# Retention and a multiplicative feed-forward block on one core: the copy of a w3 w_out tile placed behind the next tile's exponents, and the last tile of results stored in two halves

## The chip, the cores and the metric

The kernel runs on one core of a Trainium2 chip. The core has five engines with a queue of instructions each, which run side by side and wait for one another by semaphores: TensorE (PE, matmuls; its weight loads, PEld, are listed apart), VectorE (DVE), ScalarE (ACT), GpSimd (POOL) and SyncE (SP, which here issues DMAs). An instruction waits at the head of its engine's queue, and what stands behind it waits too. SBUF is the core's working memory, PSUM holds the results of matmuls in eight banks.

The metric is the device time of one execution in microseconds (us); lower is better. Inputs and outputs are in the chip's memory (HBM).

## The reference

All numbers are float32, except that the four weight matrices come as float64.

```python
scores = scale * np.matmul(q, k.transpose(0, 1, 3, 2))       # q, k, v: (8, 8, 576, 64)
rel = pos[:, None] - pos[None, :]
Dmat = np.where(rel >= 0, gamma[:, None, None] ** rel[None, :, :], 0.0)
attn = np.matmul(scores * Dmat[None], v)
x = np.ascontiguousarray(attn.transpose(0, 2, 1, 3)).reshape(B * S, H * D)   # (4608, 512)
a = x @ w1                    # w1, w2: (512, 1024)
b = x @ w2
h = a * b @ w3                # w3: (1024, 1024)
out = h @ w_out               # w_out: (1024, 512)
```

`h @ w_out` is `(a * b) @ (w3 @ w_out)`, so the kernel multiplies w3 by w_out once and uses the product, w3o (1024 x 512), for all tokens.

## The kernel before, in words

The kernel is written with a schedule by hand: each engine executes its instructions in the order in which the program issues them. Four kinds of work are interwoven.

**Attention** runs in 20 steps g (four pairs of batch entries, five chunks of the sequence each): loads of q, k and v, scaling by the decay on POOL (`scale`, L214, and `scale_blocks`, L191), transposes, scores, a running state, and `pv`, which writes tokens as columns of x^T.

**Weights.** A float64 weight arrives as pairs of 32-bit integers and is rebuilt as float32 by DVE and ScalarE, block by block. `begin_block` takes out the exponent (L370) and the mantissa (L374, L377) on DVE and has ScalarE turn the exponent into a factor with two activations (L380, L381). `end_block` puts the sign to it (L391, which needs ScalarE's result) and multiplies (L402), both on DVE. These steps are a generator, `conversion`, which begins a block before it ends the one before; `convert(n)` takes up to n steps of it, and `convert_up_to(n)` goes on until n blocks are done. A tile of w3 is two blocks; when the second is done, DVE also transposes the tile (L406) into w3T, which has three buffers. A block that has been ended makes room among five buffers for the load of a later one (`load_block`, on SP).

**The product w3 w_out** is made in eight tiles of 128 rows. `w3_mm(ft)` does tile ft: eight matmuls (each shows as two PE instructions) of w3T with `wo` into a PSUM bank `ps`, and then ScalarE's copy of the bank into `w3o` (L454). It is called from the loop at L733. While that loop has products of the first tokens to do (`todo`), they are mixed in; after that an iteration of the loop converts what is left of tile ft, calls `w3_mm(ft)`, and takes eleven more steps of conversion, which is a tile's worth. The banks `acc` are a ring of seven.

**Tokens.** `up` computes a * b for 192 positions of two batch entries in one quarter of the hidden width at a time by a Strassen scheme (seven products, whose sums DVE adds from PSUM, L502; L523 multiplies a by b). `down(x, y)` multiplies two tiles of 128 tokens, x above and y below, by w3o, in the same scheme: product 1 (A11 B11), 7 (S3 T3), 2, 6 (S2 T2), 5, 4 and 3 in this order, with sums added on DVE (L607) into `ot`, which has one buffer. S3, S2 and S1 are made on DVE at L569, L573 and L575, S4 at L628. The sums of w3o that `down` needs (T3, T2, T1, -T4) are made once, at L540, by `w3_sums`, spread over the first `up` after the product is finished. `put(m, t, row)` puts the store of one tile of tokens in a list (a tile that crosses an edge at 192 rows is stored in two pieces), and `store` issues what is listed on SP (L648). `down` calls `put` for y after product 4 and for x after product 3.

After the w3 stage, `open_attention` reuses the memory of the weight buffers, so the first loads of the next pair of batch entries wait on SP until the conversion is done. `work(n)` takes n items from the list of ups and downs; the last call, L843, empties it.

Of the kernel before, what the change touches and what calls it, by code (L numbers as in the profile page):

```python
# [40 lines left out]
def kernel(  # L41
# [13 lines left out]
    nc = tc.nc  # L55
# [3 lines left out]
    DM = H * D  # L59
    DF = moe_w3.shape[0]  # L60
    CV = 512
    P = 128
# [6 lines left out]
    NC = (S + P - 1) // P  # L69
# [3 lines left out]
    G = NB2 * NC  # L73
# [31 lines left out]
    live = {}  # L105
# [99 lines left out]
    def scale(g, nm, scalar=False):  # L205
        c = g % NC
        sz = sizes[c]
        t, gam = live[nm, g], {"q": gq, "v": gk}[nm]
        t = t[:sz].rearrange("p (b h) d -> p b h d", b=2)
        if scalar:  # L210
            for h in range(H):
                nc.scalar.mul(t[:, :, h, :], t[:, :, h, :], gam[:sz, c, h:h + 1])
            return
        nc.gpsimd.tensor_tensor(  # L214
            out=t, in0=t, in1=gam[:sz, c].unsqueeze(1).unsqueeze(3).to_broadcast([sz, 2, H, D]), op=ALU.mult)
# [214 lines left out]
    def go_on():  # L430
        while converting:
            r = next(converting[-1], "end")
            if r != "end":
                return r
            converting.pop()
        return "end"

    def convert(n):

        for _ in range(n):  # L440
            if go_on() is not None:
                return

    def convert_up_to(n):
        while converted[0] < n:
            assert go_on() is None


    def w3_mm(ft):
        ps = acc.tile([P, DM], F32, tag="acc", name="ps")  # L450
        for g in range(KF):
            nc.tensor.matmul(ps, live["w3T", ft][:, g, :], live["wo"][:, g, :],  # L452
                             start=(g == 0), stop=(g == KF - 1))
        nc.scalar.copy(live["w3o"][:, ft, :], ps)  # L454
        multiplied[0] += 1

    every = [(i, n) for i in range(NB2) for n in range(NB)]

# [123 lines left out]
    def ahead(x, y, n=3):  # L582
        todo_sums = pair_of(x, y)[2]
        for _ in range(min(n, len(todo_sums))):
            aside.append(todo_sums.pop(0))

    def down(x, y, then=None):
        for m, t in (x, y):
            if t == 2 and m % 2 == 0 and m > 0:
                assert (m, t) in carried  # L590
        a, done, left = pair_of(x, y)
        ahead(x, y)
        while len(done) < 3:
            aside.pop(0)()
        if then:
            ahead(*then)
        ps = {}
        ot = pools["ot"].tile([P, 2, 2, DM // 2], F32, tag="ot", name="ot")

        def product(nm, A, B, on=None):  # L600
            ps[nm] = ps[on] if on else acc.tile([P, DM // 2], F32, tag="acc", name="po")
            for f in range(NP):
                nc.tensor.matmul(ps[nm], a[A][:, f, :], live["W"][B][:, f, :], start=(f == 0 and not on),  # L603
                                 stop=(f == NP - 1), skip_group_check=True)

        def plus(nm, to, sb):
            nc.vector.tensor_add(ot[:, to[0], to[1]], ps[nm], ot[:, sb[0], sb[1]])  # L607

        def put(m, t, row):

            i, n = every[m]
            r0 = t * P
            while r0 < (t + 1) * P:
                b = r0 // TB
                e = min((b + 1) * TB, (t + 1) * P)
                r = (2 * i + b) * S + n * TB + r0 - b * TB
                stores.append((out[r:r + e - r0, :],
                               ot[r0 - t * P:e - t * P, row].rearrange("p h d -> p (h d)")))
                r0 = e
            if not keep_stores:  # L620
                store()

        C11, C12, C21, C22 = (0, 0), (0, 1), (1, 0), (1, 1)
        product(1, "A11", "B11")
        nc.scalar.copy(ot[:, 0, 0], ps[1])  # L625
        product(7, "S3", "T3")
        product(2, "A12", "B21", on=1)
        nc.vector.tensor_tensor(out=a["S4"], in0=a["A12"], in1=a["S2"], op=ALU.subtract)  # L628
        product(6, "S2", "T2")
        plus(6, C12, C11)  # L630
        nc.scalar.copy(ot[:, 0, 0], ps[2])
        plus(7, C21, C12)
        product(5, "S1", "T1")
        plus(5, C22, C21)
        product(4, "A22", "-T4")
        plus(4, C21, C21)
        put(*y, 1)
        product(3, "S4", "B22", on=5)
        while aside:
            aside.pop(0)()  # L640
        plus(3, C12, C12)
        put(*x, 0)

    stores, keep_stores = [], []

    def store():
        while stores:
            nc.sync.dma_start(*stores.pop(0))  # L648
# [83 lines left out]
    todo = [(0, 1, 2), (0, 0, 3), (0, 1, 3)] + [(0, 2, fp) for fp in range(NQ - 1)]  # L732
    while multiplied[0] < KF:  # L733
        ft = multiplied[0]
        done = at["w3", ft, DF // CV - 1] + 1
        ready = converted[0] >= done
        if todo:
            first = converted[0] < 4 * NQ
            up(*todo.pop(0), conv=2 if first else 1)
            convert(0 if first else 3)  # L740
        if ready or not todo:
            convert_up_to(done)
            w3_mm(ft)
        if not todo:
            convert(11)
    w3_part.close()


# [5 lines left out]
    ahead((2, 0), (2, 1), 1)  # L754
    up(0, 2, NQ - 1)
    down((2, 0), (2, 1), ((0, 0), (0, 1)))
    carry(2, 2)
    weights_part.close()
# [4 lines left out]
    keep_stores.clear()  # L763
    store()
    todo = [(down, (0, 0), (0, 1)), (down, (1, 0), (1, 1)), (down, (0, 2), (1, 2))]

    def add_pair(i):

        for n in range(NB):
            m = every.index((i, n))  # L770
            if m != NB:
                todo.append((up, i, n, 1))
            if m > NB and m % 2 == 0:
                todo.append((down, (m - 2, 2), (m - 1, 2)))
            todo.extend((up, i, n, fp) for fp in range(2, NQ))
            if m + 1 < len(every):
                todo.append((up, *every[m + 1], 0))
                if m % 2 == 0:
                    todo.append((carry, m, 2))
            else:  # L780
                todo.append((down, (m - 1, 2), (m, 2)))
            todo.append((down, (m, 0), (m, 1)))

    def work(n):
        for _ in range(min(n, len(todo))):
            fn, *args = todo.pop(0)

            nxt = next((x for x in todo if x[0] is not carry), None)
            if nxt and nxt[0] is down and fn is not carry:
                if fn is down:  # L790
                    args.append(nxt[1:])
                else:
                    last = args == [*every[max(nxt[1][0], nxt[2][0])], NQ - 1]
                    ahead(*nxt[1:], 1 if last else 3)
            fn(*args)

    scale(NC, "q")
    scale(NC, "v")
    front(NC)
# [4 lines left out]
    for g in range(NC, G):  # L804
        c = g % NC
        n = -(-len(todo) // (NC - c))
        if g + 2 < G and not in_blocks[g + 2]:
            load(g + 2, "k")
            load_blocks(g + 2, "q")
        if g + 1 < G:  # L810
            scale(g + 1, "v")
            if not in_blocks[g + 1]:
                front(g + 1, "k")
                front_blocks(g + 1, "q")
        half = (n + 1) // 2
        if in_blocks[g + 1]:
            scale_blocks(g + 1)
            work(1)
            front_blocks(g + 1)
            half = max(half - 1, 0)  # L820
        if in_blocks[g + 2]:
            load_blocks(g + 2, "q")
            load_blocks(g + 2, "k")
        work(half)
        pv(g)

        if g + 2 < G:
            queue = nc.scalar if in_blocks[g + 2] else nc.sync
            load(g + 2, "v", queue)
            if in_blocks[g + 2] and (g + 2) % NC != NC - 1:  # L830
                load(g + 2, "k", queue)
        if g + 1 < G:
            state(g + 1)
            score(g + 1)
        if g + 2 < G and not in_blocks[g + 2]:
            scale_blocks(g + 2)
        if g == NC + 1:
            strassen_tokens(1, 0)
            todo.extend((up, 1, 0, fp) for fp in range(2))
        work(n // 2)  # L840
        if c == NC - 1:
            add_pair(g // NC)
    work(len(todo))  # L843


# [41 lines left out]
```

## Time and profile before

The median of 12 runs is 863.88 us (862.36 to 865.34). The profiled execution took 862.98 us; its span, from the first to the last instruction, is 861.2 us.

| what | value |
|---|---|
| median of 12 runs | 863.88 us |
| profiled execution: own time, span | 862.98 us, 861.2 us |
| granted TensorE clock | 1.000 |
| w3 w_out stage, first to last matmul | 157.8 to 216.8 us |
| ScalarE's copies L454 in it | 8, of 587 ns |
| ScalarE's activations L380, L381 | 719 and 725 ns |
| DVE's L370, L374, L377, L391, L402 | 405, 418, 692, 687, 692 ns |
| DVE's transpose L406 | 1244 ns |
| stores of results, 256 KB and 128 KB | 24 and 24; 2.0 and 2.3 us from issue to landing |

A profile is read like this: a row of the page's groups names a line of the kernel, an engine, an operation, what it writes and reads, how many there are, their busy time and mean duration, and the idle time of the engine before them with what ended it ("<-ACT e L381": a semaphore of that instruction). The chain of waits follows the execution back from its end, at each step to what released the instruction. The work of engines that wait for something else costs no time, so the question is always which wait ends last. A matmul's end is modelled, and the mean of 596 ns for L452 counts overlapped time: they follow one another faster than that.

### The profile page before, as it was taken

What the parts mean: (1) busy time and instruction counts of PE and PEld (TensorE: products, weight loads), DVE (VectorE), ACT (ScalarE), POOL (GpSimd) and SP (SyncE); (2) the same over time, 40 slices, a digit from 0 to 9 for tenths busy, and PEclk for the clock granted to TensorE, in tenths of its full rate; (3) what the DMA queues carried; (4) which work ended last, traced back from release to release, by engine and by line L of the source; (5) the groups of instructions that cost most, each with busy time, mean ns of one, the idle gap of its engine ahead of it and who ended that gap; (6) DMA issues with size and microseconds to landing.
All of it is one profiled execution on the core that took longest, in us unless ns stands there. A gap on an engine that the chain in (4) does not pass through costs nothing.

```text
span 861.2 us, 15290 instructions
## 1 busy us (share of the span) xinstructions
PE 841.1 (98%) x6269; PEld 766.1 (89%) x6269; DVE 472.4 (55%) x794; ACT 182.1 (21%) x364; POOL 115.8 (13%) x96
## 2 busy tenths in 40 slices
PE   5899999999999999999999999999999999999998
PEld 5899999544888999999999999999999999999996
DVE  4898998986655344553544453535453334335343
ACT  3676333343122111101101101101101100001000
POOL 3010020001214213203023120230300101000000
PEclk9999999999999999999999999999999999999999
DMA  9993453455247524415241526061200000000001
GB/s 197 225 218 110 99 99 98 126 142 74 39 89 147 105 49 82 85 37 111 36 83 31 86 43 115 13 115 24 51 26 26 2 25 1 26 25 1 25 1 49
DMA packets 204918, 63.21 MB, mean 73 GB/s; under 512 B 186920, under 2 KB 195112, under 8 KB 204848
## 3 DMA queue, kind: packets, MB, share of 16 engines
q1 hardware_dynamic: 172208, 54.07, 30.3%
q10 hardware_dynamic: 32640, 8.16, 5.1%
q8 instruction: 49, 0.80, 0.4%
q14 instruction: 21, 0.17, 0.1%
HBM read 52.76 MB, written 9.44 MB: 72 GB/s over the span
## 4 chain that ended last, share of the span: by engine, by line
PE 83%; DVE 5%; DMA 2%; issue 2%; SPq 1%; ACT 1%; DVEq 0%; ACTq 0%
PE up L497 44%; PE po L603 24%; PE ps L452 4%; PE xps L300 3%; PE sc L243 3%; PE xps L293 2%; PE st L265 1%; DMA ld_q<-in_q_dram 1%; DVE c L502 1%; SPq L725 1%; PE tp L228 1%; DVE e L391 1%; DVE w L402 1%; DVE w3T L406 0%; DVE ab L523 0%
## 5 line engine op out<-in xcount | busy, mean ns | idle before, releaser
L502 DVE TENSOR_TENSOR c<-up,c 128x384 f32<-128x384 f32 x240 | 133.1, 555 | 184.8 <-PE up L497 180.1
L497 PE MATMUL up<-xT,wA 128*128 128x192 f32 x1152 | 212.1, 327 | 0.7 <-ACT xT L305 0.7
L497 PEld LDWEIGHTS up<-xT,wA 128*128 128x128 f32 x1152 | 190.7, 190 | 3.4 <-ACT xT L305 1.0
L497 PE MATMUL up<-T,wS 128*128 128x192 f32 x768 | 140.6, 326 | 2.1 <-DVE T L471 2.1
L497 PEld LDWEIGHTS up<-T,wS 128*128 128x128 f32 x768 | 127.3, 190 | 2.4 <-issue 2.4
L603 PE MATMUL po<-w3o,ab 128*128 128x256 f32 x456 | 104.3, 380 | 0.3 <-ACT ot L625 0.3
L603 PEld LDWEIGHTS po<-w3o,ab 128*128 128x128 f32 x456 | 85.8, 190 | 12.5 <-ACT ot L625 0.7
L607 DVE TENSOR_TENSOR ot<-po,ot 128x256 f32<-128x256 f32 x90 | 38.2, 424 | 75.4 <-PE po L603 72.6
L497 PE MATMUL up<-xT,wS 128*128 128x192 f32 x384 | 70.6, 327 | 0.6 <-DVE c L502 0.5
L517 ACT COPY c<-up 128x384 f32<-128x384 f32 x48 | 23.0, 479 | 226.4 <-PE up L497 222.2
L497 PE MATMUL up<-T,wA 128*128 128x192 f32 x384 | 70.2, 326 | 0.0
L246 DVE TENSOR_TENSOR pm<-sc,mask 128x512 f32<-128x512 f32 (+1 forms) x80 | 45.5, 628 | 44.8 <-PE sc L243 44.8
L603 PE MATMUL po<-wB,forms 128*128 128x256 f32 x288 | 65.2, 379 | 0.4 <-DVE forms L573 0.4
L497 PEld LDWEIGHTS up<-xT,wS 128*128 128x128 f32 x384 | 63.6, 190 | 1.5 <-DVE c L502 1.5
L497 PEld LDWEIGHTS up<-T,wA 128*128 128x128 f32 x384 | 63.7, 190 | 0.0
L603 PEld LDWEIGHTS po<-wB,forms 128*128 128x128 f32 x288 | 54.6, 190 | 8.2 <-PE po L603 0.8
L214 POOL TENSOR_TENSOR ld_v<-ld_v,gk 128x1024 f32<-128x1024 f32 (+1 forms) x17 | 33.1, 1945 | 197.8 <-DMA ld_v<-in_v_dram 161.5
L452 PE MATMUL ps<-wo,w3T 128*128 128x512 f32 x128 | 56.1, 596 | 2.9 <-DVE w3T L406 2.9
L452 PEld LDWEIGHTS ps<-wo,w3T 128*128 128x128 f32 x128 | 23.8, 190 | 34.5 <-issue 30.6
L471 POOL TENSOR_TENSOR T<-xT,T 128x384 f32<-128x384 f32 x20 | 20.8, 1042 | 218.4 <-PE up L497 216.7
L523 DVE TENSOR_TENSOR ab<-c 128x768 f32<-128x768 f32 x48 | 47.0, 978 | 3.8
L510 ACT COPY c<-up 128x384 f32<-128x384 f32 x48 | 22.9, 478 | 118.3 <-PE up L497 69.7
(73 smaller groups left out, 799.0 us busy)
## 6 DMA issues: line engine op xcount, KB each, us to landing
raw<-in_moe_w_dram SPq DMA_DIRECT2D x64, 128.0 KB, 3.0
bl_q<-in_q_dram SPq DMA_DIRECT2D x208, 32.0 KB, 2.1
out_dram<-ot SPq DMA_DIRECT2D x24, 256.0 KB, 2.0
bl_k<-in_k_dram SPq DMA_DIRECT2D x136, 32.0 KB, 2.2
raw<-in_moe_w_dram SPq DMA_DIRECT2D x8, 512.0 KB, 7.9
raw<-in_moe_w_dram SPq DMA_DIRECT2D x16, 256.0 KB, 7.1
ld_k<-in_k_dram SPq DMA_DIRECT2D x8, 512.0 KB, 7.0
ld_v<-in_v_dram SPq DMA_DIRECT2D x8, 512.0 KB, 7.2
```

Source lines behind the costliest of these rows:

```text
L214: nc.gpsimd.tensor_tensor(out=t, in0=t, in1=gam[:sz, c].unsqueeze(1).unsqueeze(3).to_broadcast([sz, 2, H, D]), op=ALU.mult)
L243: nc.tensor.matmul(sc[j][:sz, p, :sz], kT[hs, b, p, :sz], qT[hs, b, p, :sz], start=True, stop=True)
L246: nc.vector.tensor_mul(pm[:sz, b, j, :, :sz], sc[j][:sz, :, :sz], mask[:sz, :sz].unsqueeze(1).to_broadcast([sz, NP, sz]))
L300: nc.tensor.matmul(banks[r][heads[half], b, n, :sz], vs[:sz, b * H + 2 * p + j, :], pm[:sz, b, j, p, :sz], start=(c == 0 and m == 0), stop ...
L452: nc.tensor.matmul(ps, live["w3T", ft][:, g, :], live["wo"][:, g, :], start=(g == 0), stop=(g == KF - 1))
L497: nc.tensor.matmul(ps[:, w, :], a[:, w, r, :], b[:, r, :], start=(new and w == r == 0), stop=(w == r == 1), skip_group_check=True)
L502: nc.vector.tensor_add(c[:, to], ps, c[:, sb])
L510: nc.scalar.copy(c[:, 0], p1)
L517: nc.scalar.copy(c[:, 0], p1)
L523: nc.vector.tensor_mul(ab[:, 4 * fp:4 * fp + 4, :], c[:, :, 0, :], c[:, :, 1, :])
L603: nc.tensor.matmul(ps[nm], a[A][:, f, :], live["W"][B][:, f, :], start=(f == 0 and not on), stop=(f == NP - 1), skip_group_check=True)
L607: nc.vector.tensor_add(ot[:, to[0], to[1]], ps[nm], ot[:, sb[0], sb[1]])
```

## The change

`w3_mm` no longer issues the copy of its bank; it returns a function that does. The loop calls that function after the eleven steps of conversion, so the copy stands behind the instructions of those steps on ScalarE's queue. While `todo` has items, there are no such steps, and the copy is issued right after the matmuls.

`put` gets a parameter that selects columns. In the very last `down`, marked by `last=True`, the left half of x's columns is put (and so stored) after y, ahead of product 3, and the right half after product 3. In every other `down` nothing changes. The assignments to `g` serve to tell the last call.

```diff
@@ w3_mm
         for g in range(KF):
             nc.tensor.matmul(ps, live["w3T", ft][:, g, :], live["wo"][:, g, :],
                              start=(g == 0), stop=(g == KF - 1))
-        nc.scalar.copy(live["w3o"][:, ft, :], ps)
         multiplied[0] += 1
+        return lambda: nc.scalar.copy(live["w3o"][:, ft, :], ps)
@@ down
-    def down(x, y, then=None):
+    def down(x, y, then=None, last=False):
...
-        def put(m, t, row):
+        def put(m, t, row, half=slice(0, 2)):
...
-                stores.append((out[r:r + e - r0, :],
-                               ot[r0 - t * P:e - t * P, row].rearrange("p h d -> p (h d)")))
+                stores.append((out[r:r + e - r0, half.start * DM // 2:half.stop * DM // 2],
+                               ot[r0 - t * P:e - t * P, row, half].rearrange("p h d -> p (h d)")))
...
         put(*y, 1)
+        if last:
+            put(*x, 0, slice(0, 1))
         product(3, "S4", "B22", on=5)
...
-        put(*x, 0)
+        put(*x, 0, slice(1 if last else 0, 2))
@@ the loop over w3's tiles
         if ready or not todo:
             convert_up_to(done)
-            w3_mm(ft)
-        if not todo:
-            convert(11)
+            evict = w3_mm(ft)
+
+            if not todo:
+                convert(11)
+            evict()
@@ work
-            fn(*args)
-
+            if g == G and not todo:
+                fn(*args, last=True)
+            else:
+                fn(*args)
+
+    g = NC
...
+    g = G
     work(len(todo))
```

## The prediction

> **What bounds the kernel now.** I read the page first: one core, clock 1.000 in all 40 slices.
>
> ```profile
> PE 841.1 (98%) x6269; PEld 766.1 (89%) x6269; DVE 472.4 (55%) x794; ACT 182.1 (21%) x364; POOL 115.8 (13%) x96
> ```
>
> TensorE leaves little room, and a change pays only where TensorE itself stands still. So I asked next who made PE wait. The list of waits for 217 us to the end has three entries for its matmuls, 0.9 us together. For 156 to 217 us, the stage of w3 w_out, the groups by line say:
>
> ```profile
> L452 PE MATMUL ps<-wo,w3T 128*128 128x512 f32 x128 | 56.1, 596 | 2.9 <-DVE w3T L406 2.9
> L391 DVE SCALAR_TENSOR_TENSOR e<-raw,e 128x512 int32<-128x512 int32 x14 | 9.6, 687 | 2.9 <-ACT e L381 2.9
> L454 ACT COPY w3o<-ps 128x512 f32<-128x512 f32 x8 | 4.7, 587 | 36.4 <-PE ps L452 36.4
> ```
>
> PE waited 2.9 us for the transposed tile w3T, three times; DVE, which makes w3T, waited 2.9 us for ScalarE's exponents; ScalarE stood 36.4 us at the copy L454. The chain of waits (start, duration, what) joins the three:
>
> ```profile
> 164.75 1.25 DVE w3T L406
> 166.00 0.14 issue
> 166.14 7.12 PE ps L452 x16
> 173.26 0.02 issue
> 173.28 0.59 ACT w3o L454
> 173.87 0.63 ACT e L380
> 174.50 0.02 issue
> 174.52 0.73 ACT e L381
> 175.26 0.02 issue
> 175.28 0.70 DVE e L391
> ...
> 179.65 1.26 DVE w3T L406
> 180.91 0.04 issue
> 180.95 7.15 PE ps L452 x16
> ```
>
> The copy of tile 1 needs all 16 matmuls of that tile (173.26). The exponents of the next block stand behind it on ScalarE, though their input, L370, was ready at 169.15. DVE gets them 1.09 us late, tile 3's transpose is late by as much, and PE, done with tile 2 at 180.11, starts tile 3 at 180.95. It recurs at tile 5 (0.74 us of PE) and before tile 7, where PE is not waiting. PE's first wait (1.31 us, tile 1) is another: DVE is busy without a break from 157.4 to 166.0.
>
> **Part one, the copy.** The order of instructions on ScalarE in the built kernel puts the first copy behind two exponent pairs instead of none, and so on; copies 5, 6, 7 come together at the end. PE, DVE and POOL keep their order, and no DMA of the stage moves on SP. The new wait costs nothing: behind copy 1, for instance, stand the exponents of a block whose L370 ends near 176, while the copy could run from 174.7 (behind the pair of L370 at 172.74) to 175.3, its matmuls being done at 173.26. Nobody reads w3o before 219.95 (L540). The PSUM ring has seven banks; the next user of copy 1's bank is the first product after the stage.
>
> Now replay the stage. Weight loads follow each other every 0.43 us (0.19 busy, 0.24 issue), so a tile of 16 takes 6.86 when fed. A tile that waited ends 7.17 after its w3T (0.04, then 7.12 to 7.15 in the chain). So end = the later of (end before + 6.86) and (w3T + 7.17). An L391 that isn't held begins 0.61 us after L377 begins (184.43, 185.04); the three held ones began 1.78, 1.64 and 1.57 us after it: 1.17 + 1.03 + 0.96 = 3.16 us come off DVE.
>
> | tile | w3T ready, end before | w3T ready, end after |
> |---|---|---|
> | 2 | 172.82, 180.11 | 172.82, 180.12 |
> | 3 | 180.90, 188.10 | 179.73, 186.98 |
> | 4 | 187.81, 195.05 | 186.64, 193.84 |
> | 5 | 195.74, 202.94 | 193.54, 200.71 |
> | 6 | 202.72, 209.92 | 200.52, 207.69 |
> | 7 | 209.11, 216.76 | 205.95, 214.55 |
>
> **The stage ends 2.2 us earlier.** What is late next: nothing by much. DVE needs 6.8 to 7.0 us a tile and PE 6.86, so the two run neck and neck. Bounds: at most 2.34 (PE never waits after tile 1). At least 1.6: the stretches of two, two and three tiles measured 13.97, 14.10 and 20.97, where 7.12 plus 6.86 per further tile gives 13.98, 13.98, 20.84; at some 0.12 us for each of five remaining boundaries, 0.6 is lost again. I take 2.2, because the replay hits every end of before within 0.1.
>
> Raw blocks: their loads are released by L391, land after 3.0 us and are read four blocks (14 us) later, so a DVE that is 3 us ahead doesn't run dry.
>
> **What the earlier DVE sets off.** The loads of the next phase wait for its last L391 and L402 (205.68, 207.78), so they start 3.16 us earlier, and POOL's scaling with them: 0.95 us earlier seen from PE. That matters at one place.
>
> ```profile
> 228.29 2.61 POOL L214 TENSOR_TENSOR ld_v<-ld_v,gk 128x1024 f32<-128x1024 f32 x1
> 229.18 2.27 DVE L573 TENSOR_TENSOR forms<-ab 128x512 f32<-128x512 f32 x1
> ```
>
> L573 takes 0.69 elsewhere; here PE waited 0.40 for it at 231.60. Read as a proportional slowdown (3.3 times while POOL's 6.04 us from 224.86 last), DVE would lose up to 4.2 us in a worse alignment instead of today's 2.8 (L569 0.36, L523 0.85, L573 1.58), costing up to 1.4. [...] I take 0, ends -0.4 and +1.4. After that PE has no wait longer than 0.3 us to the end, so the gain goes through whole.
>
> **Part two, the last store.**
>
> ```profile
> 856.59 2.10 SPq L648 DMA_DIRECT2D out_dram<-ot  x3
> 857.86 0.43 DVE L607 TENSOR_TENSOR ot<-po,ot 128x256 f32<-128x256 f32 x1 [1.30 <-PE po L603]
> ```
>
> The 256 KB store of the upper tile leaves SP at 858.36, after the last add (858.29), and lands 2.0 later; its bytes move from 859.1 to 859.9. In the changed order SP issues the lower tile's two stores, then the first half (its data were ready at 856 or before) from about 857.7 to 858.1, by the 0.34 us of the last issue, so before the second half is ready. Only 128 KB follow the last add. If bytes set it, 0.38 us go, less some of 0.1 where the first half still moves. Against it: the lower tile's stores of 128 KB landed after 2.2 and 2.4 us, not sooner than 256 KB, so halving could cost 0.4. [...] I take 0.3, ends -0.4 (a gain) and +0.4. [...]
>
> **Sum.** 2.2 + 0 + 0.3 = 2.5 us off the profiled execution's 862.98 (span 861.2 and 1.8 around it): 860.5. The median of the runs lies 0.9 higher, 863.88, which gives **861.4**.
>
> **Rivals.**
> - *The tail gives nothing* or costs up to 0.4: the lower tile's stores still fill the engines, and the second half queues behind the first. Speaks for it: 128 KB landed no sooner. 861.7 to 862.1.
> - *DVE keeps part of it.* The neck-and-neck pace goes to DVE, or a new wait of L391 or L370 appears: 1.0 to 1.4 us in all, 862.5 to 862.9. For it: slacks of 0.1 us in the replay; against: no DVE wait but the three in the stage.
> - *No gain reaches the end*, or the copy isn't really behind the exponents: 863.9. Against: the order on ScalarE, and PE without waits behind 232.
> [...]
>
> **Numbers.** Forecast 0.66, tail 0.10, DVE 0.12, nothing 0.07, slower 0.05. The range 860.6 to 863.0 takes in the forecast's bounds and the first two rivals. About 0.2% (1.73 us) is what a measurement of this kernel can tell from no change. Faster by more: the forecast, most of the tail rival and a little of the third, 0.76. Within: the rest of these and "nothing", 0.19. Slower: 0.05.
>
> **What would show it.** Right: no DVE wait for ACT e in the stage, the copies of tiles 1 to 4 some 1.3 us after their matmuls, w3_sums' first L540 near 217.7 instead of 219.95, PE's wait for w3T only at tile 1, and a last landing near 857.9 instead of 860.4. Wrong: waits for w3T of over 0.3 us at tiles 3 to 6, a wait of PE above 1 us near 226 to 231, or a second half that lands 2.0 us or more after its issue.

## The result, and the profile after

| | before | changed |
|---|---|---|
| median of the runs | 864.01 us (862.36 to 866.34, 47 runs) | 860.96 us (860.38 to 862.7, 11 runs) |
| ratio, 95% interval | | 0.9967 [0.9959, 0.9974] |
| profiled execution: own time, span | 862.98, 861.2 us | 862.63, 860.9 us |
| tile 1's first matmul to tile 7's last | 50.62 us | 48.34 us |
| tile 7's last matmul to the start of the last add | 641.10 us | 640.85 us |
| start of the last add to the end of the span | 3.37 us | 3.34 us |

The ratio means 2.85 us less (0.0033 of 864.01), with an interval of 2.2 to 3.5; 2.5 was forecast.

The two profiled executions differ by only 0.35 us, because the one of the changed kernel lost time early. Between 33 and 40 us (columns: busy time of PE, PEld, DVE, ACT and POOL with counts, granted clock, DMA share, GB/s) the changed kernel's execution had

```profile
33.00:40.00 7.00, 6.49 (x30) 6.38 (x31) 5.71 (x13) 4.30 (x12) 0.00 (x0) 0.76 1.05 205
```

and the one of before

```profile
33.00:40.00 7.00, 6.27 (x37) 6.04 (x38) 6.94 (x15) 5.50 (x13) 0.00 (x0) 1.00 1.09 227
```

The TensorE clock granted in these 7 us was 0.76 against 1.00, which cost 1.4 us (worked out in the last section). This execution was 0.2 us ahead until then; it lost another 1.0 us in small steps between 43 and 70 us, and so the first matmul of the w3 stage came at 160.06 us instead of 157.80. None of that comes from the change, whose first edit acts in the stage. So from here on traces are compared from the stage on, and whole times only by the ratios.

The groups by line from 156 to 217 us of the changed kernel (busy us, mean ns, then idle before and who ended it) answer to the three shown of before (one L391 more falls into the same 61 us, since the stage lies 2.3 us later):

```profile
L452 PE MATMUL ps<-wo,w3T 128*128 128x512 f32 x128 | 55.4, 593 | 1.3 <-DVE w3T L406 1.3
L391 DVE SCALAR_TENSOR_TENSOR e<-raw,e 128x512 int32<-128x512 int32 x15 | 10.2, 683 | 0.0
L455 ACT COPY w3o<-ps 128x512 f32<-128x512 f32 x8 | 4.6, 572 | 11.2 <-PE ps L452 11.2
```

PE's wait for w3T has gone from 2.9 to 1.3 us, DVE's wait for the exponents from 2.9 to nothing, and ScalarE's wait at the copy (now L455) from 36.4 to 11.2 us, all of it at the last two copies, behind which no exponents stand. The chain of waits has lost its detour over ScalarE:

```profile
167.00 1.26 DVE w3T L406
168.26 0.14 issue
168.39 48.34 PE ps L452 x112
216.73 2.61 PE up L497 x16
```

112 matmuls in a row: seven tiles of 16 with nothing in between. Before, PE's rows for the same seven tiles (start, duration, wait in brackets) had two more gaps:

```profile
166.14 13.97 PE L452 MATMUL ps<-wo,w3T 128*128 128x512 f32 x32 [1.31 <-DVE w3T L406]
180.95 14.10 PE L452 MATMUL ps<-wo,w3T 128*128 128x512 f32 x32 [0.84 <-DVE w3T L406]
195.79 20.97 PE L452 MATMUL ps<-wo,w3T 128*128 128x512 f32 x48 [0.74 <-DVE w3T L406]
```

Behind the stage some of DVE's instructions take longer while POOL is scaling, as before, but not the same ones. POOL's rows:

```profile
223.62 3.62 POOL L191 TENSOR_TENSOR bl_q<-bl_q,gqs 128x512 f32<-128x512 f32 x2 [9.24 <-DMA bl_q<-in_q_dram]
227.19 2.35 POOL L214 TENSOR_TENSOR ld_v<-ld_v,gk 128x1024 f32<-128x1024 f32 x1
```

and DVE's:

```profile
224.71 1.61 DVE L540 TENSOR_TENSOR wB<-w3o,wB 128x1024 f32<-128x1024 f32 x1
226.25 0.54 DVE L502 TENSOR_TENSOR c<-up,c 128x384 f32<-128x384 f32 x1
226.71 1.07 DVE L569 TENSOR_TENSOR ab<-ab 128x512 f32<-128x512 f32 x1
227.70 2.65 DVE L523 TENSOR_TENSOR ab<-c 128x768 f32<-128x768 f32 x1
230.39 0.69 DVE L573 TENSOR_TENSOR forms<-ab 128x512 f32<-128x512 f32 x1
```

The last L540 (1.22 us elsewhere), L569 (0.68 in most other places, 1.04 here before) and L523 (0.95 elsewhere, 1.80 here before) are drawn out, while L573 (2.27 us here before) runs at its 0.69. And the end (start, duration, what):

```profile
856.31 2.24 SPq L650 DMA_DIRECT2D out_dram<-ot  x4
857.58 0.42 DVE L607 TENSOR_TENSOR ot<-po,ot 128x256 f32<-128x256 f32 x1 [1.30 <-PE po L603]
```

There are four stores where there were three; the last one lands 1.9 us after its issue instead of 2.0. The span ends 3.34 us after the last add starts, where it was 3.37 before: the half stores gave 0.03 us.

### The profile page after: what moved, and what is told of

It reads as the page before. It is cut to its first block, busy times and chain, and to the rows that moved or that the text cites. A ratio compares the mean times of both kernels' runs of the same rounds, so it can differ in the third digit from the quotient of the medians.

```text
span 860.9 us, 15292 instructions
## 1 busy us (share of the span) xinstructions
PE 841.6 (98%) x6269; PEld 767.3 (89%) x6269; DVE 473.1 (55%) x794; ACT 182.6 (21%) x364; POOL 114.7 (13%) x96
## 4 chain that ended last, share of the span: by engine, by line
PE 85%; DVE 4%; DMA 2%; issue 2%; SPq 1%; ACT 1%; DVEq 0%; ACTq 0%
PE up L497 44%; PE po L603 25%; PE ps L452 6%; PE xps L300 3%; PE sc L243 3%; PE xps L293 2%; DMA ld_q<-in_q_dram 1%; PE st L265 1%; DVE c L502 1%; PE tp L228 1%; SPq L727 0%; DVE e L391 0%; ACT ld_q L212 0%; DMA raw<-in_moe_w_out_dram 0%; DMA gqs<-decay_q_dram 0%
## 5 line engine op out<-in xcount | busy, mean ns | idle before, releaser
L497 PE MATMUL up<-xT,wA 128*128 128x192 f32 x1152 | 213.3, 328 | 1.0 <-ACT xT L305 1.0
L497 PEld LDWEIGHTS up<-xT,wA 128*128 128x128 f32 x1152 | 191.8, 191 | 3.6 <-ACT xT L305 1.3
L497 PE MATMUL up<-T,wS 128*128 128x192 f32 x768 | 141.1, 327 | 2.4 <-DVE T L471 2.1
L497 PEld LDWEIGHTS up<-T,wS 128*128 128x128 f32 x768 | 127.8, 191 | 3.0 <-issue 3.0
L497 PE MATMUL up<-xT,wS 128*128 128x192 f32 x384 | 70.6, 327 | 0.6 <-DVE c L502 0.5
L497 PE MATMUL up<-T,wA 128*128 128x192 f32 x384 | 70.3, 326 | 0.0
L497 PEld LDWEIGHTS up<-xT,wS 128*128 128x128 f32 x384 | 63.6, 190 | 1.5 <-DVE c L502 1.5
L497 PEld LDWEIGHTS up<-T,wA 128*128 128x128 f32 x384 | 63.7, 190 | 0.0
L214 POOL TENSOR_TENSOR ld_v<-ld_v,gk 128x1024 f32<-128x1024 f32 (+1 forms) x17 | 32.7, 1926 | 198.3 <-DMA ld_v<-in_v_dram 176.0
L523 DVE TENSOR_TENSOR ab<-c 128x768 f32<-128x768 f32 x48 | 48.3, 1007 | 3.8
L471 POOL TENSOR_TENSOR T<-xT,T 128x384 f32<-128x384 f32 x20 | 20.8, 1042 | 216.2 <-PE up L497 214.5
L510 ACT COPY c<-up 128x384 f32<-128x384 f32 x48 | 22.9, 478 | 118.1 <-PE up L497 69.4
```

What stands on the lines that cost most here:

```text
L214: nc.gpsimd.tensor_tensor(out=t, in0=t, in1=gam[:sz, c].unsqueeze(1).unsqueeze(3).to_broadcast([sz, 2, H, D]), op=ALU.mult)
L497: nc.tensor.matmul(ps[:, w, :], a[:, w, r, :], b[:, r, :], start=(new and w == r == 0), stop=(w == r == 1), skip_group_check=True)
L510: nc.scalar.copy(c[:, 0], p1)
L523: nc.vector.tensor_mul(ab[:, 4 * fp:4 * fp + 4, :], c[:, :, 0, :], c[:, :, 1, :])
```

## The experiments

**The copy alone, and the halves alone.** Each takes one of the two edits back:

```diff
# copy alone: the store as before
-        if last:
-            put(*x, 0, slice(0, 1))
-        put(*x, 0, slice(1 if last else 0, 2))
+        put(*x, 0)
# halves alone: the copy as before
-            evict = w3_mm(ft)
-            if not todo:
-                convert(11)
-            evict()
+            w3_mm(ft)()
+        if not todo:
+            convert(11)
```

> The copy moved behind the exponents, the last store left whole. Theory (ScalarE's queue order held DVE, DVE held PE): the stage from tile 1's first matmul to tile 7's last takes 48.3 us as in the changed kernel (50.6 before), the time falls by 2.2 to 2.4 us against before. Rival (the end of the kernel gave a good part of the 3 us that the medians moved): it falls by 1.5 to 1.9 us. By the trace: from the start of the last add L607 to the span's end 3.3 us.

> The last store in two halves, the copy left in front of the exponents. Theory of the prediction (bytes set the last store's landing): 0.3 us faster, last add to span's end 3.0 us, the second half lands 1.6 to 1.7 us after its issue. Rival (the landing is set by something other than its bytes, as the changed kernel's trace suggests with 1.9): 0 to 0.1 us, last add to span's end 3.3. A second rival (the end gave what the stage didn't): 0.6 to 0.8 us faster. The stage stays at 50.6 us.

Copy alone: 0.9974 [0.9966, 0.9983], that is 2.2 us. Its PE row (start, duration, wait in brackets) is the changed kernel's:

```profile
167.92 48.37 PE L452 MATMUL ps<-wo,w3T 128*128 128x512 f32 x112 [1.31 <-DVE w3T L406]
```

Halves alone: 0.9994 [0.9986, 1.0002], and the stage has its gaps back:

```profile
168.10 13.97 PE L452 MATMUL ps<-wo,w3T 128*128 128x512 f32 x32 [1.30 <-DVE w3T L406]
182.92 14.09 PE L452 MATMUL ps<-wo,w3T 128*128 128x512 f32 x32 [0.84 <-DVE w3T L406]
197.76 20.96 PE L452 MATMUL ps<-wo,w3T 128*128 128x512 f32 x48 [0.75 <-DVE w3T L406]
```

From the start of the last add to the end of the span the copy alone has 3.37 us, the halves alone 3.34. So the copy is the gain, and the halves gave 0.03 us. The clocked interval of the halves alone reaches from 1.2 us faster to 0.2 us slower and can't decide by itself.

**One pair of exponents ahead of the copy instead of two.**

```diff
             if not todo:
-                convert(11)
+                convert(3)
             evict()
+            if not todo:
+                convert(8)
```

> As the changed kernel, but the copy stands behind one pair of exponents instead of two. Theory: only the block whose L370 is done while the tile's matmuls still run was held by the copy; the next block's L370 ends about when the matmuls do, so its exponents behind the copy end at about 175.3 and DVE asks for them at about 176.6. The full gain, stage 48.3 to 48.5 us, no DVE wait for ACT over 0.2 us. Rival (both pairs have to be ahead, for ScalarE's time is short around the copy): DVE waits of 0.3 to 1 us per tile and half the gain or less.

0.9975 [0.9966, 0.9985], 112 matmuls in 48.41 us, and no wait of DVE for exponents. ScalarE's row shows that the copy does wait again, and harms nobody:

```profile
173.95 0.58 ACT L455 COPY w3o<-ps 128x512 f32<-128x512 f32 x1 [2.62 <-PE ps L452]
174.43 0.72 ACT L380 ACTIVATE e<-e,lim 128x512 int32<-128x512 int32 x1
```

The copy stood 2.62 us at the head of the queue, with one pair done ahead of it; the pair behind it was in time. What held DVE before was not that ScalarE waited, but that one block's exponents were behind the wait.

**Only the copies of the odd tiles behind the exponents.** In the trace of before only copies 1, 3 and 5 were followed by a wait of DVE.

```diff
             evict = w3_mm(ft)
+            if ft % 2 == 0:
+                evict()
             if not todo:
                 convert(11)
-            evict()
+            if ft % 2:
+                evict()
```

> Only the copies of tiles 1, 3 and 5 (and 7) stand behind the exponents, those of 0, 2, 4, 6 in front. In the trace of before only the copies 1, 3 and 5 were followed by DVE waits. Rival (these three copies were the guilty ones): the full gain, 2.2 us. Theory: any copy in front holds DVE when DVE is on PE's pace; copies 2 and 4 were harmless only because DVE was already late. Replayed: DVE held 1.1 to 1.2 us after copy 2 and 1.0 to 1.1 after copy 4, PE waits for w3T move to tiles 4 and 6 (0.7 to 1.1 us each), the stage ends 0 to 0.2 us earlier than before: time within 0.3 us of before.

0.9998 [0.999, 1.0006]: the stage's gain is gone, though the three copies that had been followed by waits were moved. The PE rows:

```profile
167.71 20.84 PE L452 MATMUL ps<-wo,w3T 128*128 128x512 f32 x48 [1.31 <-DVE w3T L406]
189.48 13.97 PE L452 MATMUL ps<-wo,w3T 128*128 128x512 f32 x32 [0.93 <-DVE w3T L406]
204.29 14.00 PE L452 MATMUL ps<-wo,w3T 128*128 128x512 f32 x32 [0.84 <-DVE w3T L406]
```

Tiles 1 to 3 now run through, and PE waits at tiles 4 and 6 instead of 3 and 5, with 0.93 and 0.84 us. DVE is held twice, 2.0 us together (2.1 to 2.3 were expected). From tile 1's first matmul to tile 7's last it is 50.58 us, against 50.62 before. This is the sharpest confirmation of the chain: the waits sat at every second tile only because a late DVE makes the next copy harmless.

**Quarter stores.** The halves that are finished after product 5 are stored there, so less is on its way at the end.

```diff
         plus(5, C22, C21)
+        if last:
+            put(*x, 0, slice(0, 1))
+            put(*y, 1, slice(1, 2))
         product(4, "A22", "-T4")
         plus(4, C21, C21)
-        put(*y, 1)
-        if last:
-            put(*x, 0, slice(0, 1))
+        put(*y, 1, slice(0, 1 if last else 2))
```

> The changed kernel, but in the last call the two right-hand or left-hand halves that are finished after product 5 (x left, y right) are stored there, y left after product 4, x right after product 3. In the runs so far 3.3 to 3.4 us pass from the start of the last add to the span's end with one last store or with two halves, because (theory A) the second half's bytes queue behind 384 KB that SP had issued in the 2 us before it. Here only 128 KB are issued in that time: A expects 3.0 to 3.1 us. Theory B (the time from issue to the end is set by a fixed cost, whatever the bytes): 3.3 us again. The total differs from the changed kernel by less than can be timed.

0.9970 [0.9956, 0.9984]. In the trace the span ends 3.13 us after the last add starts, near to what theory A expects. The share of the DMA engines from 856 to 862 us in 40 equal slices of 0.15 us says why. Before (last add done at 858.29):

```profile
DMA  0000000000049996988606999700000000000000
```

The changed kernel (last add done at 858.00):

```profile
DMA  0000000003998688997985962000000000000000
```

With quarters (last add done at 857.04):

```profile
DMA  0005820385001993000000000000000000000000
```

In the changed kernel the engines are still at work on what SP issued before when the last half arrives, and its last packet ends 1.74 us after the add; that of the whole store ended 1.69 us after it. With quarters the engines are idle for two slices before the last 128 KB, whose last packet ends 1.36 us after the add and which land 1.7 us after their issue.

**The last half from ScalarE's DMA queue.**

```diff
-        put(*x, 0, slice(1 if last else 0, 2))
+        put(*x, 0, slice(1 if last else 0, 2), nc.scalar if last else nc.sync)
...
```

> The changed kernel, with the very last half store issued from ScalarE's DMA queue instead of SP's. Theory A1 (the bytes queue behind the first half in SP's own queue): the engines take the two queues by turns, the last half lands earlier, 3.0 to 3.2 us from the last add to the span's end. Theory A2 (the 16 engines are busy with 384 KB whichever queue they come from) and theory B (fixed cost): 3.3 to 3.4 us. Longer than 3.4: issuing from ScalarE costs more.

0.9976 [0.9968, 0.9984]; the span ends 3.20 us after the last add starts. Here the last half leaves as soon as the add is done (at 858.09):

```profile
858.12 0.38 ACTq L650 DMA_DIRECT2D out_dram<-ot  x1
```

In the changed kernel SP is still issuing the first half when the add is done (at 858.00): of the two issues in this row the first takes 0.54 us, so the last begins only at 858.14.

```profile
857.51 1.03 SPq L650 DMA_DIRECT2D out_dram<-ot  x2
```

The four ends side by side, in us from the start of the last add, at the full resolution of the traces (other versions with one whole last store or with two halves repeat these within 0.02):

| version | last issue begins | and takes | last landing | end of the span |
|---|---|---|---|---|
| one whole store (before) | 0.49 | 0.34 | 2.48 | 3.37 |
| two halves (changed) | 0.56 | 0.40 | 2.50 | 3.34 |
| last half from ScalarE | 0.46 | 0.38 | 2.36 | 3.20 |
| quarters | 0.45 | 0.34 | 2.13 | 3.13 |

So the halves lose their gain in two ways. SP is busy with the issue of the first half: from ScalarE's queue, which is free, the last half lands 0.14 us sooner. And its bytes come behind 384 KB: counted from its issue it lands after 1.94 us from SP and after 1.90 from ScalarE, so the other queue gave 0.04 us there (theory A2), but after 1.68 with quarters, with 128 KB ahead of it. The 3.20 us lie in the range that theory A1 gave, but for another reason than its own: it is the earlier issue.

From the last landing to the end it is 0.83 us in the changed kernel, 0.90 before and 1.00 with quarters. SP's instructions at the end explain the difference: it waits for the outstanding stores one after the other, in the same order before and after, and a check whose store has landed begins 0.06 us after the one ahead of it (860.35 and 860.42 us in the trace of before). In the changed kernel the store that lands last is also the last that SP asks for; before, one more check follows, and the 1.00 us with quarters answer to three more. So of the 0.35 us by which quarters land earlier than the whole store, 0.24 arrive at the end.

**All stores after the last add**, meant as the opposite of the above:

```diff
-        put(*y, 1)
-        if last:
-            put(*x, 0, slice(0, 1))
+        if not last:
+            put(*y, 1)
...
-        put(*x, 0, slice(1 if last else 0, 2))
+        if last:
+            put(*y, 1)
+        put(*x, 0)
```

> The opposite: all three stores of the last two tiles (512 KB) are issued after the last add, whole. SP needs 0.47 + 0.53 us for the first two issues (their durations in the trace), so the last one leaves about 1.0 us later. Theory B: 3.34 + 1.0 = 4.3 us from the last add to the span's end. Theory A (bytes): the engines get 512 KB at about 260 to 430 GB/s from 0.8 us after the first issue on, 1.2 to 2.0 us, where the 256 KB before took 0.75: 3.8 to 4.6 us. It tells what early stores are worth: 0.5 to 1.2 us slower than the changed kernel.

A miss, by the way it was made. The first of the three stores still left at 856.7, when the add it reads from was done, and only the last waited for the last add (858.02): the issue stood later in the program, but SP's queue had nothing else to do, and nothing was delayed. In effect this was the copy alone once more, and it gave the same: 0.9974 [0.9966, 0.9981], 3.36 us at the end. What the early stores are worth was not tried otherwise.

**Two steps of conversion after each sum in the last up but one**, an attempt at PE's remaining 1.3 us. It was meant for the last up; but `todo.pop(0)` is evaluated before `len(todo)`, so one item is left when the last up but one is called. The last up itself kept one step.

```diff
-            up(*todo.pop(0), conv=2 if first else 1)
+            up(*todo.pop(0), conv=2 if first or len(todo) == 1 else 1)
```

> An attempt at PE's remaining wait of the stage (1.3 us for w3T of tile 1): the last up in front of the stage takes two steps of conversion after each sum instead of one. DVE has some 2 us of waits for up's products between 140 and 160. Theory: part of the conversion moves into them, tile 1's w3T comes earlier and PE's wait falls to 0 to 0.6 us, total 0.7 to 1.3 us below the changed kernel. Rival: DVE is full there, the sums L502 come later, PE waits in up for a bank or at the first product tile instead, no gain or a loss to 1 us.

1.0002 [0.9993, 1.001], so the gain of the copy is lost again. The stage itself is perfect, and what comes before it pays:

```profile
158.38 1.57 PE L497 MATMUL up<-xT,wA 128*128 128x192 f32 x8 [1.00 <-ACT c L510]
161.10 1.57 PE L497 MATMUL up<-xT,wS 128*128 128x192 f32 x8 [1.16 <-DVE c L502]
162.51 55.10 PE L452 MATMUL ps<-wo,w3T 128*128 128x512 f32 x128
```

All 128 matmuls of the stage run without a wait. But in the two ups before it PE waits 0.18, 1.00 and 1.16 us, and after the stage the wait for L569 is 1.5 us where the changed kernel has 0.3. In the outcome the rival was right. Two of the waits are for sums that DVE makes later; the one of 1.00 us is for a copy on ScalarE:

```profile
156.48 0.72 ACT L380 ACTIVATE e<-e,lim 128x512 int32<-128x512 int32 x1 [3.59 <-DVE e L370]
157.24 0.72 ACT L381 ACTIVATE e<-e,lim 128x512 int32<-128x512 int32 x1
157.87 0.46 ACT L510 COPY c<-up 128x384 f32<-128x384 f32 x1
```

L510 copies a product that was done at 152.2 us into a buffer that was free from 154.3 on (the end of L523), but it stood behind a pair of exponents whose input DVE made only by 156.4. This is the chain of this case the other way round: here the copy was ready and the exponents were not.

**The product a * b of the last up behind the stage.** DVE's L523 (0.95 us) stands among the instructions that lead to tile 1's w3T; nothing needs its result before the stage is over, and DVE then idles for 11 us.

```diff
-        nc.vector.tensor_mul(ab[:, 4 * fp:4 * fp + 4, :], c[:, :, 0, :], c[:, :, 1, :])
+        mul = lambda: nc.vector.tensor_mul(ab[:, 4 * fp:4 * fp + 4, :], c[:, :, 0, :], c[:, :, 1, :])
+        if held is None:
+            mul()
+        else:
+            held.append(mul)
...
-            up(*todo.pop(0), conv=2 if first else 1)
+            up(*todo.pop(0), conv=2 if first else 1, held=None if todo else held)
...
+    for mul in held:
+        mul()
     w3_part.close()
```

It was run together with the changed kernel and with a version that has the quarter stores too.

> The changed kernel once more, on the same chip as the two that follow. If its lead over the copy alone (2.9 us against 2.2 us by the ratios) is chance, it comes out at 2.2 to 2.5 us below before; if the half stores are worth 0.6 us, at 2.8 or more.

> The changed kernel; the product a * b of the last up in front of the stage (L523, 0.95 us of DVE, of which 0.87 until the next instruction starts) goes behind the stage's conversion, where DVE stands idle for 11 us. Theory: DVE's pace sets the start of tile 1, and from there DVE and PE run level, so all w3T come 0.87 us earlier, PE's wait at tile 1 falls from 1.31 to 0.4 to 0.5 us, and the stage, first matmul of tile 0 to the last of tile 7, from 56.7 to 55.8 us: 0.9 us faster than the changed kernel. Rival: the gain is lost again behind the stage (w3T takes its buffers, or the wait for L569 grows): 0 to 0.4 us.

> Both of the above and the four quarter stores of the last call: 0.9 us from the stage, and 3.2 us from the last add to the end where the changed kernel has 3.3: 1.0 us below the changed kernel, 3.3 to 3.6 below before.

The changed kernel came out at 0.9967 [0.9956, 0.9979] again, 2.9 us. With the product moved it is 0.9962 [0.995, 0.9975], with the quarters as well 0.9954 [0.994, 0.9967], 4.0 us below before. The intervals overlap, so the order of the three is not shown by the clock. The trace shows the stage's part:

```profile
158.48 7.03 PE L452 MATMUL ps<-wo,w3T 128*128 128x512 f32 x16
166.08 48.34 PE L452 MATMUL ps<-wo,w3T 128*128 128x512 f32 x112 [0.57 <-DVE w3T L406]
```

PE's wait at tile 1 fell from 1.31 to 0.57 us, and from the first matmul of tile 0 to the last of tile 7 it is 55.94 us (214.42 less 158.48) where the changed kernel has 56.67: 0.73 of the 0.87 expected. Behind the stage nothing of it is lost: the wait for S3 (L569, L573 in this version's count of lines) stays at 0.3 us. The version with both has 3.14 us at the end, as the quarters alone have 3.13.

## Why the prediction was right, and where not

- **What bounds the kernel**: right. PE's waits in the stage were worth what they showed. The chain from the copy over the exponents, DVE and w3T to PE is shown by three runs: it goes with the copy alone, it comes back with the copy in front, and it moves to the tiles where the replay put it when every second copy is in front.
- **The stage, 2.2 us**: it measured 2.28 (50.62 less 48.34), between the forecast and the upper bound of 2.34. The replay had DVE and PE neck and neck with DVE ahead of need by hundredths of a microsecond at some tiles; in the trace PE never waits after tile 1. The lower bound of 1.6, which charged 0.12 us for each boundary, was too careful.
- **The cover of the new wait**: right, and more than was needed; one pair of exponents ahead does as well as two.
- **What the earlier DVE sets off, 0**: it was a gain of 0.25 us. The last matmul of the stage to the last add takes 641.10 us in the kernel of before and 641.11 with the halves alone, and 640.85 to 640.86 in the copy alone, the one-pair version, the odd copies and both profiles of the changed kernel. All of it comes off by 232 us. No run shows the 0 of the forecast; in its place the traces show that the last L540 (1.61 us), L569 (1.07) and L523 (2.65) are now drawn out while L573 takes its 0.69, and that PE waits at product 7 for L569 (0.28 us) where it had waited at product 6 for L573 (0.40). Counted from the end of the stage, L569 ends 0.4 us later than before and L573 0.3 us earlier. POOL's L191 and L214 run at the same time as the three that are drawn out; that they are the cause is read from this overlap and was not tried by itself.
- **The last store, 0.3 us**: wrong, it gave 0.03. Two terms failed. One is "less some of 0.1 where the first half still moves": the bytes of the last half ended no sooner after the last add than those of the undivided store (1.74 us against 1.69), since 384 KB had been put on the same engines ahead of them. The other is that SP would be done with the first half's issue before the second half is ready, "by the 0.34 us of the last issue": that issue took 0.54 us, and the last one began 0.07 us later than before. With both out of the way, as with quarters, the landing came down from 1.99 us after the issue to 1.68: 0.31 us for 128 KB less, where half of the 0.75 us in which the undivided store's bytes moved would be 0.38. The rival "the tail gives nothing" was right for this part, and for the reason it named.
- **The sum**: 2.28 + 0.25 + 0.03 is 2.56, and 2.5 was forecast. That the two agree so well is luck, for two misses of about 0.3 cancelled. The clock says 2.85 [2.2, 3.5], twice nearly the same figure, and 2.2 for the copy alone. Whether the 0.3 us beyond the traces are real is open, but the runs speak against it when they are sorted by their granted clock (last section): at 0.998 the second set of the changed kernel has a median 2.2 us below that of before (4 runs against 9), and the copy alone 2.1 us (4 against 20).
- **Slower, 0.05**: didn't happen. POOL's scaling behind the stage took 5.9 us (223.62 to 229.54), against 6.04 before, and PE's one wait for DVE there fell from 0.40 to 0.28 us.

## What to carry to other kernels

A copy out of PSUM that waits for matmuls belongs behind whatever on the same in-order queue is ready sooner and feeds a busier engine (here worth 2.2 us); look for the instruction behind the wait, not for the wait. The order pays only while what is put ahead is ready sooner: where exponents that were not ready stood ahead of a copy, PE waited 1.0 us for the copy. Where two engines run at the same pace (here 6.8 to 7.0 us a tile for DVE and 6.86 for PE), a wait that shows at every second step can be a wait of every step: moving only the copies that show it gained nothing here (0.9998), so replay the whole stretch tile by tile. Halving the last store gave 0.03 us, with 384 KB ahead of the last half and SP still at an issue of 0.54 us when it was ready; storing the parts as they were finished gave 0.24.

## What the runs showed that was not expected

The mean granted clock of TensorE was 0.998 in 10 of the 13 profiled executions and 0.999 or 1.000 in the other three. In the changed kernel's it fell to half once while TensorE was at work, and early. Slice by slice of 1 us (the clock is the third number from the end):

```profile
34.00:35.00 1.00, 1.00 (x7) 0.87 (x5) 1.00 (x3) 1.00 (x5) 0.00 (x0) 0.79 1.10 252
35.00:36.00 1.00, 1.00 (x5) 0.99 (x4) 1.00 (x3) 0.36 (x2) 0.00 (x0) 0.50 1.06 182
36.00:37.00 1.00, 1.00 (x5) 1.00 (x4) 0.69 (x3) 0.60 (x1) 0.00 (x0) 0.50 1.04 154
37.00:38.00 1.00, 1.00 (x4) 1.00 (x4) 0.02 (x1) 0.84 (x2) 0.00 (x0) 0.51 1.11 277
```

It came after PE had waited 2.1 us for DVE (`T`, L471) until 33.5 us. What it cost can be read from the rows around it: the products with wS behind that wait (L497) began 0.22 us sooner than in the execution of before (33.51 against 33.73), the transposes of k (L228) behind the dip 1.22 us later (43.06 against 41.84), so 1.4 us, half of what this change brings. The clocked runs say the same. Those of before, taken beside the experiments on the last store, fall into 15 with a mean clock of 1.000 and a median of 863.48 us and 22 with 0.998 and 864.86 us, 1.4 us apart.

In the changed kernel's trace the clock falls at 34.57 us, 10.24 us after the trace's record of it begins, and is back at 37.98, 3.41 us later. That is 1.72 us of clock lost between 33 and 40 us; in seven more of the ten executions (the copy alone, the halves alone, one pair, the odd copies, two steps of conversion, the changed kernel's second profile and the product behind the stage) the same 7 us lost 1.69 to 1.73 us of clock. What decides whether it falls is not shown: the same wait of 2.1 us stands at the same place in executions without a dip (2.09 us before, 2.09 with product and quarters). The version with product and quarters lost time before the stage all the same (0.8 us at the weight sums wS, 0.7 at the scaled q), so the clock is not the only source of the spread between runs. PE waited 1.0 and 2.1 us ahead of the dip; to fill these waits was not tried.
